# Selective attention and a routed expert layer: the diagonal half blocks of keys in 64 by 64 tiles

## The chip, the cores and the metric

The kernel runs on one core of a Trainium2 chip. A core has five engines, each with a queue of its own: TensorE multiplies matrices (a weight load, then a matmul that streams the moving operand past the weights), VectorE and ScalarE work element by element, GpSimd does masks and indirect stores, and SyncE issues most transfers. The engines wait for each other at semaphores. The results of matmuls land in PSUM; the attention here uses three buffers of two banks and two single banks of it, a bank being 512 fp32 columns on 128 partitions. All other tiles lie in SBUF, 128 partitions wide.

The metric is the device time of the whole kernel in microseconds (us), given as the median of the runs. Beside it stands one execution that the hardware profiler recorded; its span runs from the first to the last instruction. All data is fp32, and an fp32 product appears in the trace as two records of a weight load and a matmul.

## The reference

Inputs have 8 batches, 8 heads, 576 positions and head size 64. The first half is causal attention with a bias from a running sum of a score `s`:

```python
scores = scale * np.matmul(q, k.transpose(0, 1, 3, 2))
causal = np.triu(np.ones((S, S), dtype=bool), k=1)
cum = np.cumsum(np.maximum(s, 0.0), axis=-1)
bias = -(cum[:, :, :, None] - cum[:, :, None, :])
scores = np.where(causal, -1e9, scores + np.minimum(bias, 0.0))
attn = np.exp(scores - np.max(scores, axis=-1, keepdims=True))
attn = attn / (np.sum(attn, axis=-1, keepdims=True) + 1e-09)
out = np.matmul(attn, v)
```

Its output, 8 x 576 tokens of width 512, goes into a routed layer. Each token has logits over 8 experts; a local gate says whether it takes the expert of its own largest logit or that of the token before it. The token then gets `relu(x @ w1[e]) @ w2[e]` (512 to 1024 to 512), times its probability of that expert.

## The kernel before

**Two stages.** `attention` (L764) computes all of the attention, and between its pieces the routing of batches that are complete. `Experts.run` (L647) then goes through the tokens sorted by expert. A fallback for inputs out of range (`attention_general` and what follows it) is built into the program and does not run on this input.

**Pairs and slots.** A unit of attention is n: one batch and two heads, 32 in all. The two heads lie on partitions 0 to 63 and 64 to 127 of q and k. The main loop (L1000) takes two n at a time, the first (a) and the second (b); I call one turn of it a slot, 0 to 15. In a slot TensorE does four score units of a, four of b, then the values of a, then those of b.

**Scores.** Keys are taken in chunks of 128 (c = 0 to 3, and NF = 4 for the last 64). A chunk needs only queries from its own first position on. `UNITS` (L40) says which chunks make up a unit, with query ranges and the place of each in the unit; `WIDTH` gives 384, 384, 448 and 384 columns per head. `scores` (L891) issues for each piece one product per head: contraction over 64 partitions, 128 keys as output rows. The result is in one of three PSUM buffers of two banks (`ps_s`, L779), one bank per head. One exponential on ScalarE (L903) takes the unit to SBUF (`e`), and `masked` (L887) on GpSimd zeroes what lies above the diagonal.

**Values.** Queries are taken in blocks of 64 (j = 0 to 8). For block j, `values` (L922) adds over all chunks c up to the diagonal: `e` of 64 queries as weights, contraction over 128 keys, and as moving operand the weighted values `vg`, 66 columns wide (64 values, the key weight for the row's sum, and ones). A head's output goes to half of the partitions. Blocks whose diagonal chunk is only half filled (j even) still contract over all 128 keys: the upper half of the weights was set to zero. Blocks 0 to 5 and 6 to 8 (`NJA = 6`) have one bank each, from the pool `ps_o` (L780), which both n of a pair share. `evacuate` on VectorE divides by the row's sum (a reciprocal, L939, and a multiply, L940).

**What sets the order.** The program's order is kept as it is written, on every engine. A tile of a pool waits for the last reader of the tile that had its buffer before. `at(m, place)` (L996) runs work that was planned for slot m: places 0 and 1 come after the scores of a and b, 3 and 4 after their values, 5 at the slot's end. The router's steps are planned there (L965): `product` at place 1 of slots 4, 8 and 12, `logits` at 3, `codes` and `turn1` at 5; in the slot after, `turn2` at 3; in the next one `ranks` (the matmuls called pos) at 1, `rows` and `gates` at 3. `assign_early` is at place 3 of slot 11. Stores to a table in memory (`scatter`, L339) are spread over places 0 to 5 of later slots; some wait on GpSimd for a reciprocal of a value block.

**Loads.** `load_qk` (L788) fetches q and k of one n. In slot m it is issued, after the first n's values, for the pair two slots on, with a small copy on ScalarE to hold it back. `load_v` fetches values six n ahead; `weigh` (L874) multiplies them by the key weights, one slot ahead, on VectorE. Key weights (`key_weights`, L857) are made once in slot 0.

Of the kernel before, what the change touches and what calls it, by code (L numbers as in the profile page):

```python
# [9 lines left out]
F32 = mybir.dt.float32  # L10
I32 = mybir.dt.int32
Act = mybir.ActivationFunctionType
Alu = mybir.AluOpType
# [22 lines left out]
NJ = S // DH  # L36
NJA = 6
G1 = 2
REF = (127, 415)
UNITS = (((0, 0, 384, 0),), ((0, 384, S, 0), (3, 384, S, 192)), ((1, P, S, 0),), ((2, 256, S, 0), (NF, TS, S, 320)))  # L40
WIDTH = (384, 384, 448, 384)
GB = 2
# [8 lines left out]
BX = 3  # L51
FIRST = ((0, P, 0, 3 * P), (P, S, 3 * P, S))
CAP = N + DH
# [710 lines left out]
def attention(ctx, tc, q, k, v, s, wx, ident, recs, wend, router, experts):  # L764
# [4 lines left out]
    def pool(name, bufs, **kw):  # L769
        return ctx.enter_context(tc.tile_pool(name=name, bufs=bufs, **kw))  # L770
# [3 lines left out]
    p_v = pool("p_v", NVA)  # L774
    p_e = pool("p_e", 2)
    p_x = experts.p_x
    p_x0 = pool("p_x0", 1)
# [6 lines left out]

    ins, vs, es, xs, xts = {}, {}, {}, {}, {}
    heads = [slice(DH * h, DH * h + DH) for h in range(2)]

    def load_qk(n, behind=None):  # L788

        if n >= NPAIR:  # L790
            return
        b, hp = divmod(n, HP)
        ins[n] = qb, kb = p_in.tile([P, S], F32, name="qb"), p_in.tile([P, S], F32, name="kb")
        if behind is not None:
            nc.scalar.copy(kb[0:1, 0:1], behind)
        for k0, k1, q0, q1 in FIRST if n == 0 else ((0, S, 0, S),):
            nc.sync.dma_start(kb[:, k0:k1], k[b][:, hp, k0:k1])
            nc.sync.dma_start(qb[:, q0:q1], q[b][:, hp, q0:q1])

# [28 lines left out]
    wk = once.tile([P, NPAIR, G1 + NB, 2], F32, name="wk")  # L828
    nc.gpsimd.memset(wk[:TL, :, G1 + NF], 0.0)
    for t in vgs:  # L830
        nc.gpsimd.memset(t[..., VW - 1 : VW], 1.0)
        nc.gpsimd.memset(t[:TL, G1 + NF, :, VW - 1 : VW], 0.0)

# [18 lines left out]
    def key_weights():  # L852
        cps = banks("cps")[:, 0].rearrange("p (i n) -> p i n", n=B * H)
        i = 0
        for w, n in ((w1, G1), (w2, NB)):
            for c in range(n):
                a = min(c * P, S - P)  # L857
                tr(cps[:, i], w[:, a : a + P], ident[: B * H, : B * H])
                i += 1
        for i in range(G1 + NB):  # L860
            d = slice(TL if i == G1 + NF else 0, P)
            nc.vector.tensor_copy(wk[d, :, i, :].rearrange("p n h -> p h n"), cps[d, i].rearrange("p (h n) -> p h n", h=2))

# [22 lines left out]

    def masked(ap, n, base=0):  # L887
        nc.gpsimd.affine_select(out=ap, in_=ap, compare_op=Alu.is_ge, fill=0.0, base=base, pattern=n,  # L888
                                channel_multiplier=-1)

    def scores(n, u):  # L891
        if n >= NPAIR:
            return
        qb, kb = ins[n]
        if u == 0:
            es[n] = [p_e.tile([P, 2, w], F32, name=f"e{i}") for i, w in enumerate(WIDTH)]
        e = es[n][u]
        ps = banks("ps")[:, :, : WIDTH[u]]
        for c, a, z, at in UNITS[u]:
            key = min(c * P, S - P)  # L900
            for h, d in enumerate(heads):
                mm(ps[:, h, at : at + z - a], lhsT=kb[d, key : key + P], rhs=qb[d, a:z], start=True, stop=True)  # L902
        nc.scalar.activation(e, ps, Act.Exp, scale=scale)  # L903
        for c, a, z, at in UNITS[u]:
            m = min(P, z - a)
            if a < c * P + P:
                masked(e[:, :, at : at + m], [[0, 2], [1, m]], P - m)

# [12 lines left out]

    def values(n, j0, j1):  # L922
        b, hp = divmod(n, HP)
        if b not in xs:
            xs[b] = x_tile(b) if b < BX else p_x.tile([P, NJ, 2, XW], F32, name="xb")
        xb = xs[b]
        po = ps_o.tile([P, j1 - j0, VW], F32, name=f"po{j0}")
        for j in range(j0, j1):
            last = j // 2 if j < NJ - 1 else NF
            for c in range(last + 1):  # L930
                for h, d in enumerate(heads):
                    mm(po[d, j - j0, :], lhsT=weights_of(n, c, j, h),  # L932
                       rhs=vgs[n % NV][:, c if j < 2 * G1 else G1 + c, h, :],
                       start=(c == 0), stop=(c == last))

        def evacuate():
            m = j1 - j0
            rec = recs[:, n, j0:j1, :]
            nc.vector.reciprocal(rec, po[:, :, VW - 2 : VW])  # L939
            nc.vector.tensor_tensor(xb[:, j0:j1, :, 32 * hp : 32 * hp + 32], po[:, :, :DH].rearrange("p j (g i) -> p j g i", g=2),  # L940
                                    rec[:, :, 0].unsqueeze(2).unsqueeze(3).to_broadcast([P, m, 2, 32]), op=Alu.mult)

        return evacuate, po[0:1, 0, 0:1]

# [51 lines left out]
    def at(slot, place):  # L996
        for f in todo.pop((slot, place), ()):
            f()

    for m in range(NPAIR // 2):  # L1000
        pair = 2 * m, 2 * m + 1
        for n in pair:
            for u in range(len(UNITS)):
                if (n, u) == (0, 2):
                    key_exps()
                scores(n, u)
                if (n, u) == (0, 3):
                    key_weights()
                    weigh(0)
                    weigh(1)  # L1010
                if (n % 2, u) == (1, 1):
                    load_v(n - 1 + NVA, es[n][u][0:1, 0, 0:1])
                    load_v(n + NVA)
            at(m, n - 2 * m)
        for n in pair:
            values(n, 0, NJA)[0]()
            evacuate, done = values(n, NJA, NJ)
            if n % 2 == 0:
                load_qk(n + NV, done)
                load_qk(n + 1 + NV)  # L1020
            evacuate()
            at(m, 3 + n - 2 * m)
        last = m % HP == HP - 1
        if last:
            turns(pair)
        for n in range(WEIGHED[m - 1] + 1 if m else 2, WEIGHED[m] + 1):
            weigh(n)
        if not last:
            turns(pair)
        at(m, 5)  # L1030
# [36 lines left out]
def attention_general(ctx, tc, q, k, v, s, w_gate, w_local, cum_d, x_d, ident, lg):  # L1067
# [24 lines left out]
    def load_batch(b):  # L1092
        if b >= B:
            return
        qb = p_in.tile([P, HP, S], F32, name="qb")
        kb = p_in.tile([P, HP, S], F32, name="kb")
        vb = p_in.tile([P, NF, H, DH], F32, name="vb")
        vl = p_in.tile([TL, H, DH], F32, name="vl")
        nc.sync.dma_start(qb, q[b])
        nc.sync.dma_start(kb, k[b])  # L1100
        for hp in range(HP):
            hs = slice(2 * hp, 2 * hp + 2)
            nc.sync.dma_start(vb[:, :, hs], v[b, hp][:, :NF])
            nc.sync.dma_start(vl[:, hs], v[b, hp][TL:, NF])
        ins[b] = qb, kb, vb, vl
# [500 lines left out]
```

## Time and profile before

| what | us |
|---|---|
| median of 3 runs | 747.14 (745.63 to 747.15) |
| profiled execution, whole | 731.85 |
| its span, first to last instruction | 730.1 |
| sixteen slots of attention, first score to last value | 4.8 to 209.4 |
| experts, to the end | 209.4 to 730 |

The profile's busy row of an engine is the time in which it had at least one instruction under way; matmuls overlap, so TensorE at 98% is not TensorE at its peak. The chain of waits follows the work that ended last backwards from the end. Rows of groups give line, engine, operation, tiles, the shape, the count, the busy time and the mean length of one in ns. `64*128` in such a row is a matmul on 64 partitions with 128 weight columns, `128*64` one on 128 partitions with 64.

In the ten slices of the span that hold the attention, VectorE is busy 40 to 80%, ScalarE 30 to 50%, GpSimd 30 to 80%:

```profile
DVE  4656678778865751101111401420041001050010
ACT  5554555363521101101101011101101011101110
POOL 3453467688583534510010101010001001010110
```

The exponentials, masks and evacuations of the attention are these groups:

```profile
L903 ACT ACTIVATE e<-ps 128x768 f32<-128x768 f32 (+1 forms) x128 | 96.5, 839 | 47.2 <-PE ps L902 42.3
L888 POOL TENSOR_SCALAR_AFFINE_SELECT e<-e 128x256 f32<-128x256 f32 (+1 forms) x160 | 67.2, 445 | 50.4 <-ACT e L903 49.5
L939 DVE RECIPROCAL recs<-po 128x12 f32<-128x12 f32 x64 | 13.4, 210 | 51.4 <-PE po L932 39.9
```

### The profile page before, as it was taken

The page shows a single profiled execution, that of the slowest core. Times are in us where ns is not written, and L with a number is a line of the kernel's source. Part 1 is how long each engine was busy: PE and PEld are TensorE (multiplying, and loading weights), DVE is VectorE, ACT ScalarE, POOL GpSimd, SP SyncE. Part 2 cuts the span into 40 slices and gives each one's busy share as a digit, 9 for nine tenths or more (in the row PEclk, how much of TensorE's full clock was granted, in tenths as well). Part 3 has the DMA queues.
Part 4 walks back from the last instruction along what each step waited for, and adds up shares of the span by engine and source line. Part 5 has one row for each costly group of instructions (what it writes and reads, how often), then busy time and mean ns, then how long its engine had stood idle before and what let it go on. Part 6 is the DMA issues. An engine that isn't in the chain of part 4 may idle for free.

```text
span 730.1 us, 16198 instructions
## 1 busy us (share of the span) xinstructions
PE 719.0 (98%) x6521; PEld 496.6 (68%) x6521; DVE 258.4 (35%) x713; ACT 165.4 (23%) x355; POOL 206.1 (28%) x453
## 2 busy tenths in 40 slices
PE   8999999999999999999999999999999999999996
PEld 7888888878886766756765377446736576646673
DVE  4656678778865751101111401420041001050010
ACT  5554555363521101101101011101101011101110
POOL 3453467688583534510010101010001001010110
PEclk9999999999999999999999999999999999999998
DMA  8455465765749997887457969996999964997000
GB/s 305 153 173 170 142 197 172 219 207 184 216 150 424 343 384 263 320 331 221 151 210 243 399 256 426 311 381 261 388 363 374 389 240 176 341 410 288 30 17 32
DMA packets 57205, 187.28 MB, mean 257 GB/s; under 512 B 11838, under 2 KB 32062, under 8 KB 49569
## 3 DMA queue, kind: packets, MB, share of 16 engines
q1 hardware_dynamic: 50224, 165.91, 63.7%
q0 software_dynamic: 6800, 20.09, 7.2%
q8 instruction: 53, 0.87, 0.5%
q14 instruction: 32, 0.25, 0.1%
q10 hardware_dynamic: 96, 0.15, 0.1%
HBM read 165.50 MB, written 20.75 MB: 255 GB/s over the span
## 4 chain that ended last, share of the span: by engine, by line
PE 96%; DMA 1%; ACT 1%; DVE 1%; issue 1%; POOL 0%; POOLq 0%; DVEq 0%; ACTq 0%
PE yp L634 35%; PE hp L608 31%; PE po L932 12%; PE ps L902 11%; PE hp L599 4%; PE lp L217 1%; DMA table<-xb,idx 1%; ACT e L903 1%; PE warm L837 1%; DVE xb L940 0%; PE pos L301 0%; POOL e L888 0%; POOL table L349 0%; PE pos L302 0%; DVE y L637 0%
## 5 line engine op out<-in xcount | busy, mean ns | idle before, releaser
L634 PE MATMUL yp<-w2b,hT 128*128 128x512 f32 (+3 forms) x752 | 259.3, 593 | 0.0
L608 PE MATMUL hp<-xT,w1b 128*128 128x256 f32 (+2 forms) x1216 | 229.8, 349 | 0.0
L608 PEld LDWEIGHTS hp<-xT,w1b 128*128 128x128 f32 x1216 | 206.2, 190 | 29.3 <-issue 7.5
L634 PEld LDWEIGHTS yp<-w2b,hT 128*128 128x128 f32 (+3 forms) x752 | 107.1, 166 | 141.8 <-issue 140.2
L639 POOL DMA_INDIRECT out_dram<-y,gi x37 | 36.4, 984 | 413.2 <-DVE y L637 387.3
L610 ACT ACTIVATE hT<-hp 128x256 f32<-128x256 f32 (+2 forms) x152 | 53.4, 352 | 425.4 <-PE hp L608 425.4
L637 DVE TENSOR_SCALAR y<-yp,gi 128x512 f32<-128x512 f32 (+1 forms) x37 | 27.6, 745 | 304.8 <-PE yp L634 298.5
L903 ACT ACTIVATE e<-ps 128x768 f32<-128x768 f32 (+1 forms) x128 | 96.5, 839 | 47.2 <-PE ps L902 42.3
L932 PE MATMUL po<-vg,e 128*64 128x66 f32 x3200 | 98.5, 223 | 2.2 <-issue 1.2
L932 PEld LDWEIGHTS po<-vg,e 128*64 128x64 f32 x3200 | 95.5, 138 | 5.1 <-issue 3.7
L902 PE MATMUL ps<-qb,kb 64*128 64x192 f32 (+4 forms) x768 | 94.1, 397 | 0.5 <-ACT e L903 0.3
L902 PEld LDWEIGHTS ps<-qb,kb 64*128 64x128 f32 x768 | 64.9, 187 | 28.8 <-ACT e L903 16.3
L888 POOL TENSOR_SCALAR_AFFINE_SELECT e<-e 128x256 f32<-128x256 f32 (+1 forms) x160 | 67.2, 445 | 50.4 <-ACT e L903 49.5
L349 POOL DMA_INDIRECT table<-xb,idx x54 | 54.2, 1003 | 17.1 <-issue 13.3
L619 DVE STREAM_TRANSPOSE hT<-hs 32x256 f32<-32x256 f32 x64 | 27.9, 436 | 72.3 <-ACT hs L601 71.4
L882 DVE TENSOR_TENSOR vg<-va,wk 128x256 f32<-128x256 f32 x64 | 41.7, 716 | 0.0
L939 DVE RECIPROCAL recs<-po 128x12 f32<-128x12 f32 x64 | 13.4, 210 | 51.4 <-PE po L932 39.9
L599 PE MATMUL hp<-w1b,xT 128*32 128x512 f32 (+1 forms) x224 | 28.3, 594 | 0.0
L578 DVE STREAM_TRANSPOSE xT<-xq 128x1024 f32<-128x1024 f32 (+1 forms) x23 | 23.6, 1028 | 12.0 <-DMA xq<-table 11.6
L940 DVE TENSOR_TENSOR xb<-po,recs 128x384 f32<-128x384 f32 (+1 forms) x48 | 22.0, 458 | 2.4 <-DMA table<-xb,idx 0.8
L599 PEld LDWEIGHTS hp<-w1b,xT 128*32 128x32 f32 (+1 forms) x224 | 8.1, 114 | 17.6 <-issue 17.5
L951 DVE STREAM_TRANSPOSE xt<-xb 128x576 f32<-128x576 f32 x24 | 17.1, 751 | 0.0
(254 smaller groups left out, 200.8 us busy)
## 6 DMA issues: line engine op xcount, KB each, us to landing
w2b<-in_w_dram SPq DMA_DIRECT2D x30, 2048.0 KB, 12.8
w1b<-in_w_dram SPq DMA_DIRECT2D x29, 2048.0 KB, 10.1
va<-in_v_dram SPq DMA_DIRECT2D x32, 320.0 KB, 4.2
kb<-in_k_dram SPq DMA_DIRECT2D x31, 288.0 KB, 3.4
qb<-in_q_dram SPq DMA_DIRECT2D x31, 288.0 KB, 4.9
xq<-table SPq DMA_DIRECT2D x56, 130.0 KB, 8.6
w1b<-in_w_dram SPq DMA_DIRECT2D x4, 512.0 KB, 5.2
xq<-table SPq DMA_DIRECT2D x20, 65.0 KB, 11.0
```

The source lines that it names most:

```text
L349: put = self.nc.gpsimd.indirect_dma_start(out=self.halves, in_=src, element_offset=0, in_offset=None, out_offset=bass.IndirectOffsetOnAxis ...
L599: mm(ps[d, :], lhsT=xT[:, k, d], rhs=self.ws[l][0][:, k, c * 512 : c * 512 + 512], start=(k == 0), stop=(k == DK - 1))
L608: mm(ps[:, :w], lhsT=self.ws[ls[0]][0][:, k, c * P : c * P + P], rhs=xT[:, k, :w], start=(k == 0), stop=(k == DK - 1))
L610: nc.scalar.activation(self.hT[u][:, c, :w], ps[:, :w], Act.Relu)
L619: self.nc.vector.transpose(hT[32 * a : 32 * a + 32, :, 32 * r : 32 * r + 32], hs[32 * r : 32 * r + 32].rearrange("p (c i) -> p c i", i=P)[ ...
L634: mm(ps[d, :], lhsT=hT[:, k, n * P + d.start : n * P + d.stop], rhs=self.ws[l][1][:, k, :], start=(k == 0), stop=(k == FK - 1))
L639: put = nc.gpsimd.indirect_dma_start(out=self.out[:, :], out_offset=bass.IndirectOffsetOnAxis(ap=gi.bitcast(I32)[:m, n, 0:1], axis=0), in_ ...
L882: nc.vector.tensor_tensor(vg[:, to].rearrange("p c h e -> p (c h) e")[:, :, :DH], va[:, :c].rearrange("p c h e -> p (c h) e"), wk[:, n, to ...
L888: nc.gpsimd.affine_select(out=ap, in_=ap, compare_op=Alu.is_ge, fill=0.0, base=base, pattern=n, channel_multiplier=-1)
L902: mm(ps[:, h, at : at + z - a], lhsT=kb[d, key : key + P], rhs=qb[d, a:z], start=True, stop=True)
L903: nc.scalar.activation(e, ps, Act.Exp, scale=scale)
L932: mm(po[d, j - j0, :], lhsT=weights_of(n, c, j, h), rhs=vgs[n % NV][:, c if j < 2 * G1 else G1 + c, h, :], start=(c == 0), stop=(c == last))
```

## The change

The keys are put into another order, made where the inputs are laid out: block 8 first, then 0, 1, 2, 3, 5, 4, 7, 6. A chunk of 128 keys now starts at 64, so chunk c holds blocks 2c and 2c + 1 (for c = 2 and 3 in swapped places). The whole chunk is computed only for queries from block 2c + 1 on. For query block 2c itself only half of the chunk counts, its diagonal half block of 64 keys; for blocks 0, 2, 4 and 6 that half is computed apart, as 64 by 64 tiles, with blocks 0 and 4, and 2 and 6, side by side on the two halves of the partitions (`HALVES`).

- Scores: three units per n in place of four (512, 448 and 384 columns; chunk queries start 64 later), and one more unit of 256 columns per pair for the half blocks of both n (`scores_halves`), with one exponential and two masks. It is issued in the slot before the one that uses it, between the values of a and of b.
- Values: whole chunks contract over 128 keys as before; the four half blocks contract over 64 (`values_halves`). The halves of a close its accumulation, those of b open it, so both stand together.
- Banks: the values of a stay in `ps_o`; those of b go to a buffer of `ps_s`. Blocks are split into 0 to 3 and 4 to 8 (`NJA = 4`).
- Order in a slot: scores of a and b; whole values of a, its halves, halves of b, half scores of the next pair; evacuation of a; the loads; place 3; then the whole values of b.
- In slot 0 the first loads are cut differently, the key weights are turned after the third unit, and chunks with swapped blocks take two copies (nine in place of seven).

```diff
-NJA = 6
+NJA = 4
-UNITS = (((0, 0, 384, 0),), ((0, 384, S, 0), (3, 384, S, 192)), ((1, P, S, 0),), ((2, 256, S, 0), (NF, TS, S, 320)))
-WIDTH = (384, 384, 448, 384)
+BLOCKS = (8, 0, 1, 2, 3, 5, 4, 7, 6)
+UNITS = (((0, DH, S, 0),), ((1, 3 * DH, S, DH), (NF, TS, S, 0)), ((2, 5 * DH, S, 0), (3, 7 * DH, S, 256)))
+WIDTH = (512, 448, 384)
+TURNED = (2, 3)
+ROOM = (512, 448, 512)
+HALVES = ((0, 4), (2, 6))
...
+    p_eh = pool("p_eh", 1)
...
         for i in range(G1 + NB):
-            d = slice(TL if i == G1 + NF else 0, P)
-            nc.vector.tensor_copy(wk[d, :, i, :].rearrange("p n h -> p h n"), cps[d, i].rearrange("p (h n) -> p h n", h=2))
+            d = slice(0, P)
+            c = i - G1
+            for to, of in (heads[:2],) if c == NF else (heads, heads[::-1]) if c in TURNED else ((d, d),):
+                nc.vector.tensor_copy(wk[to, :, i, :].rearrange("p n h -> p h n"),
+                                      cps[of, i].rearrange("p (h n) -> p h n", h=2))
...
+    def scores_halves(m, ps):
+        if 2 * m >= NPAIR:
+            return
+        eh[m] = p_eh.tile([P, 2, 2, len(HALVES), DH], F32, name="eh")
+        ps = ps[:, :, : 4 * DH]
+        for i in range(2):
+            qb, kb = ins[2 * m + i]
+            for t, blocks in enumerate(HALVES):
+                for side, x in zip(heads, blocks):
+                    at = (2 * i + t) * DH
+                    key = BLOCKS.index(x) * DH
+                    for h, d in enumerate(heads):
+                        mm(ps[side, h, at : at + DH], lhsT=kb[d, key : key + DH], rhs=qb[d, x * DH : x * DH + DH],
+                           start=True, stop=True)
+        nc.scalar.activation(eh[m].rearrange("p h n t i -> p h (n t i)"), ps, Act.Exp, scale=scale)
+        by = eh[m].rearrange("p h n t i -> p (h n t) i")
+        masked(by[:DH], [[0, 8], [1, DH]])
+        masked(by, [[0, 8], [1, DH]], DH)
...
+    def room(n):
+        if n % 2:
+            po = banks("pb")
+            po = [po[:, i] for i in range(2)]
+        else:
+            po = [ps_o.tile([P, 512], F32, name=f"po{i}") for i in range(2)]
+        return [ps[:, : (z - a) * VW].rearrange("p (j w) -> p j w", w=VW) for ps, (a, z) in zip(po, PARTS)]
+
+    def values(n, po, part, first, last):
+        a, z = PARTS[part]
+        steps = [(j, c) for j in range(a, z) for c in [*range((j + 1) // 2), *([NF] if j == NJ - 1 else [])]]
+        for i, (j, c) in enumerate(steps):
+            for h, d in enumerate(heads):
+                mm(po[part][d, j - a, :], lhsT=weights_of(n, c, j, h),
+                   rhs=vgs[n % NV][:, c if j < 2 * G1 else G1 + c, h, :],
+                   start=(first and i == 0), stop=(last and i == len(steps) - 1))
+
+    def values_halves(n, po, first):
+        e = eh[n // 2][:, :, n % 2]
+        for t, blocks in enumerate(HALVES):
+            for part, (side, j) in enumerate(zip(heads, blocks)):
+                for h, d in enumerate(heads):
+                    mm(po[part][d, j - PARTS[part][0], :], lhsT=e[side, h, t],
+                       rhs=vgs[n % NV][side, j // 2 + (G1 if part else 0), h, :],
+                       start=(first and t == 0), stop=(not first and t == 1))
...
-        for n in pair:
-            values(n, 0, NJA)[0]()
-            evacuate, done = values(n, NJA, NJ)
-            if n % 2 == 0:
-                load_qk(n + NV, done)
-                load_qk(n + 1 + NV)
-            evacuate()
-            at(m, 3 + n - 2 * m)
+        a, b = pair
+        po = room(a)
+        for i in range(2):
+            values(a, po, i, True, False)
+        values_halves(a, po, False)
+        halves = banks("ph") if b + 1 < NPAIR else None
+        to = room(b)
+        values_halves(b, to, True)
+        scores_halves(m + 1, halves)
+        evacuate(a, po, 0)
+        load_qk(a + NV, po[1][0:1, 0, 0:1])
+        load_qk(b + NV)
+        evacuate(a, po, 1)
+        at(m, 3)
+        for i in range(2):
+            values(b, to, i, False, True)
+            evacuate(b, to, i)
+        at(m, 4)
```

## The prediction

> **What bounds the kernel now.** I read the page's busy rows first, then the chain of waits, then the groups with shapes kept apart, last VectorE's timeline and TensorE's waits.
>
> ```profile
> span 730.1 us, 16198 instructions
> PE 719.0 (98%) x6521; PEld 496.6 (68%) x6521; DVE 258.4 (35%) x713; ACT 165.4 (23%) x355; POOL 206.1 (28%) x453
> ...
> PE   8999999999999999999999999999999999999996
> ```
>
> TensorE is busy from end to end, at full clock. A busy TensorE can still hide slack, so the chain between 61 and 89 us has to show a rhythm:
>
> ```profile
> 61.70 2.31 PE lp L217 x64
> 64.01 5.98 PE po L932 x200
> 69.99 5.76 PE ps L902 x48
> 75.75 5.98 PE po L932 x200
> 81.74 5.76 PE ps L902 x48
> ```
>
> A slot (one pair of n) is 5.76 us of scores and 5.98 us of values, 11.74 in all, and nothing else ends last. Sixteen slots fill 4.8 to 209.4 us; the experts after them are not edited, and TensorE is busy 513.8 of their 520.6 us. So the change is worth what it does to TensorE's 11.74 us per slot, plus any wait it opens. The groups give the unit prices:
>
> ```profile
> L634 PE MATMUL yp<-w2b,hT 128*128 128x512 f32 x464 | 202.8, 593 | 0.0
> L932 PEld LDWEIGHTS po<-vg,e 128*64 128x64 f32 x3200 | 95.5, 138 | 5.1 <-issue 3.7 <-POOL e L888 0.7
> L902 PEld LDWEIGHTS ps<-qb,kb 64*128 64x128 f32 x768 | 64.9, 187 | 28.8 <-ACT e L903 16.3 <-issue 0.7 <-DMA qb<-in_q_dram 0.6
> L217 PEld LDWEIGHTS lp<-xt,wx 128*32 128x32 f32 x320 | 8.6, 110 | 0.8 <-issue 0.3
> L217 PE MATMUL lp<-xt,wx 128*32 128x160 f32 x192 | 7.1, 300 | 0.0
> ```
>
> An fp32 product is two records. A whole-array record of 512 columns costs 202.8/464 = 437 ns, 0.854 ns a column. The values phase has 200 x 66 columns, 11.3 us at that price, and takes 5.98: two column tiles run at once. Scores: 12,800 columns, 10.9 us, in 5.76: two row tiles at once. The router's product: 64 x 160 columns, 8.7 us, in 2.31: 3.8 tiles at once.
>
> **What the Trainium skill says.** "TensorEngine Tiling (Array Packing)", Tiling Modes: 64 by 64 is four independent tiles, and changing the mode drains TensorE. The trace shows the drain: from the starts of single records, the last score to the first value is 202 ns and the next start 108, where 49 and 58 are the rhythm: 0.20 us; values to scores likewise 0.20. It shows no 64 by 64 tile. "TensorE: Matmul & The Clock Gate", LDWEIGHTS: time goes with columns, P/1.2 ns; the records agree (187, 138, 110 ns for 128, 64, 32 columns: 0.8 ns each). Its Back-to-back issue gap gives a floor of about 25 ns a matmul; the trace differs, records of different tiles start 6 to 7 ns apart. "PSUM — Partial Sum Buffer", PSUM bank collisions: row tiles may not share a bank; the change keeps each row tile in its own bank, so this costs nothing.
>
> **The change, part by part.** Rhythm of two tiles, from starts: 0.84 ns a column and record for wide scores, 58.4 ns for a values step of 66 columns, 112 ns where a 64-column score has 128 weights to load (56 before, but the next step is late by as much).
>
> *Scores before*: per n 1,536 wide columns x 2 x 0.84 = 2.58 us, and 0.11 to 0.22 for the 64: 5.50 a pair. *After*: 512+384+256+128 = 1,280 columns x 2 x 0.84 = 2.15, the 64-wide 0.22: 2.37 per n, 4.75 a pair. Saved 0.75.
>
> *Half scores*: 16 products a pair, 32 records of 64 columns. Four at a time that is 8 steps of 56 ns, 0.45 us; two at a time 0.90. I take four: column tiles show 3.8, row tiles 1.9, each with its own weight loads in parallel, and the router's four products stand in the program in the same way.
>
> *Values before*: 25 (block, chunk) steps per n, 50 a pair x 2 x 58.4 = 5.84. *After*: 21 whole per n, 42 x 2 x 58.4 = 4.91, and 16 half products: 8 steps, 0.47 (0.93 if only two tiles run). Saved 0.46.
>
> *Switches*: two a slot become four (scores, values of a, halves, values of b). I take 0.17 us for each new one: the lp to values switch cost 0.16, the dear ones 0.20; bounds 0.10 and 0.25.
>
> Sum of an ordinary slot: 4.75+0.45+4.91+0.47+0.40+0.34 = 11.32 against 5.50+5.84+0.40 = 11.74: **0.42 us less**. Slots 1 to 14: 5.9. Slot 15 computes no next halves: 0.87. Slot 0 computes two sets of halves with two more switches (+0.79), and its halves reuse the bank pair of the transposed key weights, whose copies grow from 7 to 9 (about 0.17 us each): +0.3. With its own 0.42 off, slot 0 loses 0.7. TensorE: **-6.1 us**.
>
> *New wait*. The values of the second n leave ps_o for one of the three score buffers. The third score unit of the next slot takes that buffer, so it waits for the last evacuation, on VectorE, behind whatever the router has at place 3. An evacuation pair takes 1.31 us. In after's slot, with 0 at its first score, the first n's evacuation can start at 7.98, and the second's last multiply must end by 11.31+1.73 = 13.0 (1.73 us are the first two units). That leaves 2.2 us for place 3. The timeline of before:
>
> ```profile
> 79.56 0.70 DVE L278 COPY ei<-exm 32x18 f32<-32x18 f32 x4
> ...
> 82.22 0.21 DVE L939 RECIPROCAL recs<-po 128x12 f32<-128x12 f32 x1
> ...
> 92.01 0.30 DVE L310 TENSOR_TENSOR at<-pos,base 128x144 f32<-128x144 f32 x1
> ...
> 94.92 0.23 DVE L939 RECIPROCAL recs<-po 128x12 f32<-128x12 f32 x1
> ...
> 154.74 0.16 DVE L366 TENSOR_TENSOR cnt<-base,base 128x8 int32<-128x8 f32 x1
> ...
> 157.51 0.23 DVE L939 RECIPROCAL recs<-po 128x12 f32<-128x12 f32 x1
> ```
>
> turn2 takes 2.7 us (slots 5, 9, 13), rows and gates 2.9 to 3.1 (slots 6, 10, 14), assign_early 2.8 (slot 11); logits, 2.2, just fit (slots 4, 8, 12). Over the 2.2: 0.5, 0.8, 0.6. In slots 9 and 13 codes and turn1 of the slot before run until about 8.5, 0.5 more. Together 3 x 0.5 + 2 x 0.5 + 3 x 0.8 + 0.6 = **+5.7 us** (I round up by 0.2 for the semaphores). Queued behind the waiting matmul is all of TensorE. Bounds: 0 if VectorE runs ahead of my sum, 9 if it runs 0.5 later in the seven slots.
>
> *Waits that go*. Values of the second n now have banks of their own, so they no longer wait for the first n's evacuation:
>
> ```profile
> PE po L932 <- DVE xb L940: 0.3, 1, 0.3
> PE po L932 <- DVE recs L939: 0.2, 1, 0.2
> ```
>
> The starts show three such gaps, at 128.7, 179.8 and 192.9 us: 1.2 us over the rhythm. Next in line there is the wait just priced. Slot 11 loses 0.7 us at 150 to 157 us, mostly to masks behind two stores on GpSimd; I take half back, 0.35, since the stores stay.
>
> *At nothing*. ScalarE: exponentials start every 0.70 (768) and 0.81 us (896), so 0.93, 0.81, 0.70 and 0.47 a half set: 5.35 a slot, 5.82 before; the three buffers cover its small lag behind TensorE (2.44 against 2.37 per n). GpSimd: ten masks (3.9 us in a quiet slot) become six plus two of 512 elements; from 0.29 and 0.34 us for 128 and 256 these take 0.45, up to 1.0 when contended: 3 to 4.5, read a slot later. On its queue they now stand ahead of place 3's store, which waits for the first n's reciprocal anyway. SyncE: the same q, k and v bytes; the next pair's q and k are wanted at 7.9 us in the slot after their issue at about 9, after 10 us, and land in some 7 (four, at medians of 3.4 and 4.9). If that cover fails, the halves wait up to 2 us a slot. The key and value orders are made outside the timed program.
>
> Sum: -6.1 + 5.7 - 1.2 - 0.35 = **-1.95 us**. The profiled execution would go from 731.85 (span 730.1) to about 729.9. The median of the runs is 747.14, 15.3 us more, which no view explains; I take it as fixed: **745.2 us**.
>
> **The rivals.**
> 1. *No late VectorE.* The evacuation always meets its limit: -6.1-1.2-0.35 = -7.7, 739.5 us. For it: VectorE is busy only 6.4 to 9.1 us of the five slots I asked for, 11.8 to 14 us long. Against: the sums above are of measured lengths, in order.
> 2. *Halves two at a time (slower).* The half products cost 0.92 us a slot more, 15 us in all. They delay the second values by 0.68, so the late evacuation shrinks to 1.1. Sum -6.1+15+1.1-1.2-0.35 = +8.4: 755.5 us. It decides once the halves cost 0.19 us a slot more (16 steps of 57 ns, 0.92 us, become 1.1), so below about 3.3 tiles of 4 at once. For it: no 64 by 64 tile in the trace, and weights of 64 columns need as long as their matmul. Against: rows and columns each pack.
> 3. *The buffer wait everywhere.* With one of three buffers held until a slot's end, TensorE, ScalarE and VectorE run in lockstep and most slots lose 0.3 more, or the new switches cost 0.25: +4.5 on the forecast, 749.7 us. For it: ScalarE is as slow as TensorE in the scores. Against: in a plain slot the last evacuation ends 0.87 us after the scores start and is wanted at 1.73.
>
> That the change does not do what it says is excluded: the changed order on TensorE has 16 products of 64x64 and 16 half values a slot, and the third unit waits on VectorE.
>
> **How the numbers follow.** Forecast 0.44 (742.5 to 747.5), rival 1 0.14, rival 2 0.18, rival 3 0.24. No change means within 0.2%, 1.5 us. Faster: 0.33 + 0.14 + 0.01 = 0.48; same: 0.08 + 0.05 = 0.13; slower: 0.03 + 0.18 + 0.18 = 0.39. The range reaches to half of rivals 1 and 2: 740 to 755.5.
>
> **What would show it.** In quiet slots (1 to 3) the chain should repeat every 11.3 us: scores 4.75, first values 2.45, halves 1.1 with both products, second values 2.45. Halves of 2 us mean rival 2. In slots 6, 7, 10, 11, 12, 14 and 15 the first record of the third score unit should start 0.5 to 1 us late, released by VectorE; without that it is rival 1. A shortfall in quiet slots too is rival 3. Wrong altogether if the experts' stretch, 520.6 us, changes.

## The result, and the profile after

| | before | changed kernel |
|---|---|---|
| median of 6 runs each, us | 746.48 (745.56 to 747.15) | 813.11 (811.04 to 814.43) |
| ratio to before | 1 | 1.088, 95% interval 1.087 to 1.090 |
| profiled span, us | 730.1 | 812.5 |
| attention ends, first expert product (us of the span) | 209.6 | 289.7 |

The change costs 66.6 us where 2 us of gain were forecast. The kernel before itself takes 746 to 747 us in some sets of runs and 730 to 731 in others (its profile is like the latter), so every kernel below is set against the runs of before in its own set.

The page of the changed kernel, its header, TensorE's busy row and slices, and the clock it was granted:

```profile
span 812.5 us, 16822 instructions
...
PE 742.6 (91%) x6909; PEld 512.3 (63%) x6909; DVE 255.0 (31%) x715; ACT 157.8 (19%) x339; POOL 202.2 (25%) x421
...
PE   8987778777777789999999999999999999999996
...
PEclk9999889989888999999999999999999999999999
```

The loss lies in the first 15 slices, which are the attention. There TensorE is mostly seven to eight tenths busy where it had been full, and its clock falls too. The rest, 522.8 us from 289.7 to the end, is close to the 520.5 of before.

The chain of waits of the changed kernel, over the end of slot 2 and the start of slot 3, two quiet slots (start, length, engine, tile):

```profile
46.16 0.60 ACT eh L937
46.81 0.23 DVE recs L992
47.07 0.49 DVE w2b L993
47.71 0.44 DVE w2b L993
48.19 2.20 PE pb L972 x68
50.39 4.96 PE ps L913 x40
55.35 2.60 PE po L972 x84
57.95 0.39 PE po L982 x16
58.35 0.23 PE pb L982 x16
58.58 0.69 PE ph L935 x32
```

Before, this chain held TensorE alone, scores and values in turn. Now the second half of every slot goes ScalarE, VectorE, TensorE. In the 84 records of the second values (L972, `pb`), the first 16 run at once; the other 68, which are part 1, start only after an evacuation (L993). TensorE's waits say the same:

```profile
PE pb L972 <- DVE xb L993: 48.0, 12, 4.7
PE pb L972 <- DVE w2b L993: 3.1, 2, 1.7
PE pb L972 <- DVE w1b L993: 3.0, 2, 1.5
```

Sixteen waits, one a slot, 54.1 us. (`xb`, `w1b` and `w2b` are the same output tiles under different names.) Measured from the starts of single records, the gap before part 1 is 1.6 to 1.8 us in the five slots without router work for VectorE at place 3 and 3.5 to 4.8 us in the other eleven, 56.7 us in all. Slot 6 in the timeline shows what is in such a gap:

```profile
109.14 0.69 PE L972 MATMUL pb<-vg,e 128*64 128x66 f32 x16
109.77 0.13 ACT L800 COPY kb<-po 1x1 f32<-1x1 f32 x1
109.94 0.22 DVE L992 RECIPROCAL recs<-po 128x10 f32<-128x10 f32 x1 [0.72 <-ACT kb L800]
110.60 0.30 DVE L314 TENSOR_TENSOR at<-pos,base 128x144 f32<-128x144 f32 x1
...
113.72 0.20 DVE L992 RECIPROCAL recs<-pb 128x8 f32<-128x8 f32 x1
113.96 0.42 DVE L993 TENSOR_TENSOR xb<-pb,recs 128x256 f32<-128x256 f32 x1
114.44 4.01 PE L972 MATMUL pb<-vg,e 128*64 128x66 f32 x68 [4.61 <-DVE xb L993]
```

Part 0 of b is done by 109.8. Its evacuation stands on VectorE behind the evacuation of a and then behind the router's rows and gates (L314 to L340), so it ends at 114.4. Part 1 of b starts at 114.44, directly after it, although it writes the other bank. Then those 68 records last 4.01 us instead of the 2.2 of the quiet slot. The windows of these two stretches give the reason (stretch, length, busy time of the engines, then the granted clock, DMA share, GB/s):

```profile
core 0: us, PE busy (x) PEld busy (x) DVE busy (x) ACT busy (x) POOL busy (x), PEclk, DMA share, GB/s
...
114.40:118.30 3.90, 3.86 (x68) 3.82 (x68) 0.00 (x0) 0.00 (x0) 0.00 (x0) 0.50 0.05 17
118.30:124.00 5.70, 5.70 (x46) 3.64 (x44) 4.20 (x8) 3.88 (x5) 3.59 (x7) 0.89 0.07 23
```

After the wait TensorE runs at half clock for the whole of part 1 and into the scores. "TensorE: Matmul & The Clock Gate" of the Trainium skill, in its part on the HAM clock gate, says that the clock drops to half after an idle window of some 3.4 us. The trace agrees with the length of the window: the second values lose 1.3 to 1.8 us more after each of the eleven long waits, 3.46 us and up, and the half clock starts at times that are whole multiples of 3.41 us apart (20.58, 78.61, 95.67 us and so on) and lasts 3.41 or 6.83 us.

But here the window need not be idle all through. Of the five short waits, slot 0's is followed by the half clock as well (its half scores had halted 0.8 us just before): in the 3.41 us up to 20.58 TensorE was busy for 1.49. If this trace's attention is cut into such windows, every one with 1.92 us or more of idle time is followed by half clock; those at full clock with less, 1.66 us at most, are not. Three of the other short waits are followed by nothing of the kind, and slot 7's second values hold two other stalls of 0.6 us. All together it is 20.6 us in the second values, 1.3 of them in slot 7, and 2.9 in the scores.

So 56.7 + 20.6 + 2.9 = 80.2 us lost, against 7.7 us of forecast gains (6.1 on TensorE, 1.55 in waits): 72.5. The two spans differ by 82.4 us. Of the 10 between, 2.3 lie in the experts and some 7 in short stalls of TensorE, of a kind that before's profile does not have (last section). The medians differ by only 66.6, because before's own runs beside it took 15 us more than its profile; no trace shows where they spend them.

### The profile page after: what moved, and what is told of

Read it like the earlier page. It is cut to its first block, busy times and chain, and to the rows that moved or that the text cites. A ratio compares the mean times of both kernels' runs of the same rounds, so it can differ in the third digit from the quotient of the medians.

```text
span 812.5 us, 16822 instructions
## 1 busy us (share of the span) xinstructions
PE 742.6 (91%) x6909; PEld 512.3 (63%) x6909; DVE 255.0 (31%) x715; ACT 157.8 (19%) x339; POOL 202.2 (25%) x421
## 4 chain that ended last, share of the span: by engine, by line
PE 89%; DVE 7%; issue 2%; ACT 1%; DMA 0%; SPq 0%; POOL 0%; POOLq 0%; DVEq 0%; ACTq 0%
PE yp L638 32%; PE hp L612 28%; PE ps L913 10%; PE pb L972 7%; PE po L972 5%; PE hp L603 3%; DVE xb L993 1%; PE lp L221 1%; PE ph L935 1%; ACT eh L937 1%; PE po L982 1%; DVE l L236 1%; DVE recs L992 1%; DMA va<-in_v_dram 0%; PE pb L982 0%
## 5 line engine op out<-in xcount | busy, mean ns | idle before, releaser
L972 PE MATMUL pb<-vg,e 128*64 128x66 f32 x1344 | 65.9, 276 | 54.9 <-DVE xb L993 48.0
L914 ACT ACTIVATE e<-ps 128x1024 f32<-128x1024 f32 (+2 forms) x96 | 80.8, 924 | 97.9 <-PE ps L913 97.9
L972 PEld LDWEIGHTS pb<-vg,e 128*64 128x64 f32 x1344 | 60.7, 187 | 58.5 <-DVE xb L993 49.6
L913 PE MATMUL ps<-qb,kb 64*128 64x64 f32 (+5 forms) x644 | 84.9, 415 | 0.8 <-ACT e L914 0.8
L913 PEld LDWEIGHTS ps<-qb,kb 64*128 64x128 f32 x644 | 55.1, 194 | 29.1 <-issue 8.2
L897 POOL TENSOR_SCALAR_AFFINE_SELECT e<-e 128x128 f32<-128x128 f32 (+2 forms) x96 | 40.8, 435 | 65.8 <-ACT e L914 65.1
L972 PE MATMUL po<-vg,e 128*64 128x66 f32 x1344 | 44.3, 224 | 1.0 <-issue 0.8
L972 PEld LDWEIGHTS po<-vg,e 128*64 128x64 f32 x1344 | 41.4, 138 | 4.1 <-issue 2.7
L992 DVE RECIPROCAL recs<-po 128x8 f32<-128x8 f32 (+1 forms) x32 | 6.8, 214 | 77.6 <-PE po L982 65.3
L897 POOL TENSOR_SCALAR_AFFINE_SELECT eh<-eh 64x512 f32<-64x512 f32 (+1 forms) x32 | 21.0, 656 | 38.8 <-ACT kb L800 33.4
```

What stands on the lines that cost most here:

```text
L914: nc.scalar.activation(e[:, :, : WIDTH[u]], ps, Act.Exp, scale=scale)
L972: mm(po[part][d, j - a, :], lhsT=weights_of(n, c, j, h), rhs=vgs[n % NV][:, c if j < 2 * G1 else G1 + c, h, :], start=(first and i == 0), ...
```

## The experiments

The theory: part 0 and part 1 of b lie in one tile of two banks (`banks("pb")`), and the program has `evacuate(b, to, 0)` ahead of `values(b, to, 1)`; so part 1, a writer of the tile, waits for the reader of part 0, whichever bank that reads. The rivals: the half blocks themselves, their masks, or the held score buffer cause the stall.

**Both evacuations last.** The order alone is changed.

```diff
         for i in range(2):
             values(b, to, i, False, True)
+        for i in range(2):
             evacuate(b, to, i)
```

> The changed kernel with one move: both parts of the second n's values are issued before both of its evacuations. Theory A, one tile: in the changed kernel the second part (68 records) waits for the evacuation of the first part, because both parts lie in one two-bank tile and that evacuation stands ahead of them; the waits add up to some 56 us and the halved clock after them to some 20 us. So A expects 736 to 743 us here: second values 2.45 us in quiet slots (4.15 before the move), clock 0.99 or more, and at most 6 us of new waits of the third score unit for VectorE. Theory B, the held score buffer: giving one of three score buffers to the values until the slot's end is what costs; then 790 us or more, with the waits at the score units. Theory C, VectorE is simply late: the wait moves from the values to the next slot's third score unit and the time stays above 790 us.

Measured: 739.56 us (738.57 to 741.1) beside 730.68 of before; ratio 1.0129, interval 1.0112 to 1.0146. The second values take 2.45 us in nine of the sixteen slots and at most 3.6 in the rest, the granted clock is 0.999 over the span, and most of the loss has gone. That 739.56 lies in the expected 736 to 743 is luck: these numbers stood against 747 of before and meant 4 to 11 us less than it, and it is 8.9 more. The mechanism held; the new wait, at most 6 us expected, is larger. It is the one that the prediction had priced:

```profile
PE ps L913 <- DVE xb L993: 10.5, 10, 1.8
```

Ten score phases are late, by 0.6 to 2.0 us over their 4.76, 12.6 us in all; 5.7 us in seven slots were forecast. The chain of this kernel at slot 9's end tells why it is more (pieces as before, some left out):

```profile
132.05 0.60 ACT eh L937
132.65 0.04 ACT kb L800
...
132.71 0.23 DVE recs L992
...
132.97 0.49 DVE xb L993
133.46 0.07 DVE ei L282
...
136.07 0.47 DVE incl L297
...
137.26 0.50 DVE xb L993
...
137.90 3.31 PE ps L913 x28
```

The second evacuation of a (132.71) waits for the one-element copy of L800, which `load_qk` places on ScalarE between the two evacuations of a; and that copy is queued behind the exponential of the half scores. The pair that the sum had at 1.31 us runs from 131.12, in the timeline, to 133.46: 2.34 us; in the other slots before a late score phase it takes 2.13 to 2.52, but in slot 14 1.58. "PSUM — Partial Sum Buffer" of the Trainium skill, in the section on bank collisions, tells of a scheduler that adds a dependency between two engines on one bank and quarter of the partitions, reads included; this copy and this evacuation are such a pair, both reading bank po1. The trace shows that the evacuation waits for the copy; that this rule put the wait there is not shown.

**The kernel before, with both parts of its values in one tile of two banks.** No half blocks, no held score buffer: only the suspected cause.

```diff
-        po = ps_o.tile([P, j1 - j0, VW], F32, name=f"po{j0}")
+        if j0 == 0:
+            pos[n] = ps_o.tile([P, 2, 512], F32, name="po")
+        po = pos[n][:, int(j0 > 0), : (j1 - j0) * VW].rearrange("p (j w) -> p j w", w=VW)
```

> The kernel before, with both parts of an n's values in one tile of two banks instead of a tile each; nothing else is changed. Theory A: the second part of every n waits for the evacuation of the first, about 1.1 us (0.17 drain, 0.23 and 0.56 on VectorE, 0.14 to release), 35 us over 32 n; the second n's first part waits for the first n's last evacuation, about 1.2 us, 19 us; and in the eleven slots with router work at place 3 the second n's wait is 2 to 3 us longer, some 25 us. Sum about 825 us, and in any case over 780. Theories B and C have no wait here that was not there before: 750 us at most.

Measured: 795.96 us beside 730.68 (one run). The tile alone costs the kernel before 65 us. Its waits:

```profile
PE po L934 <- DVE xb L942: 40.5, 35, 1.9
PE po L934 <- DVE w1b L942: 5.6, 6, 1.0
PE po L934 <- DVE w2b L942: 4.7, 5, 1.0
```

Here both n of a pair have such a tile, so there are 46 waits, none over 1.9 us. The kind is right; the amount is below the 78 us expected, since the longer waits expected in the slots with router work did not come.

**The changed kernel with the router behind.** Evacuation 0 of b is moved ahead of place 3; the tile stays one.

```diff
-        at(m, 3)
-        for i in range(2):
-            values(b, to, i, False, True)
-            evacuate(b, to, i)
+        values(b, to, 0, False, True)
+        evacuate(b, to, 0)
+        at(m, 3)
+        values(b, to, 1, False, True)
+        evacuate(b, to, 1)
```

> The changed kernel with place 3 (the router's work on VectorE) moved from ahead of the second n's first values and their evacuation to behind them; VectorE has the same work. Theory A: the second part still waits for the evacuation of the first, but about 1.7 us in every slot as in the quiet ones, and no wait is long enough to halve the clock: 760 to 770 us, clock 0.99 or more. Theory C: VectorE's load is the same, so 800 us or more. Theory B: no difference, 813 us.

Measured: 748.52 us beside 730.68 (one run), 17.8 more than before; 13 to 23 more were expected (the numbers there stand against 747). TensorE's waits:

```profile
PE pb L972 <- DVE xb L993: 17.1, 12, 1.7
PE pb L972 <- DVE w1b L993: 3.0, 2, 1.5
PE pb L972 <- DVE w2b L993: 3.0, 2, 1.5
```

Sixteen waits are left, but now every slot has the quiet slot's, 1.1 to 1.9 us by the starts of records, 25.7 in all. No second values run at the lowered clock: part 1 takes the quiet slot's 2.13 us in all sixteen slots, so nothing is left of the 20.6 us. So the place of the router's work decides between 1.7 us and 4.8, and with the long waits the lowered clock goes too.

**Where the third unit's wait comes from.** Three kernels on top of "both evacuations last", and the changed kernel itself beside them. The first moves the loads of q and k:

```diff
-        load_qk(a + NV, po[1][0:1, 0, 0:1])
-        load_qk(b + NV)
         evacuate(a, po, 1)
+        load_qk(a + NV, po[1][0:1, 0, 0:1])
+        load_qk(b + NV)
```

> As the kernel with both of the second n's evacuations last (ratio 1.013 to before; third score unit late by 12.6 us in all), but the loads of the next q and k, whose one-element copy on ScalarE stands between the two evacuations of the first n and holds VectorE idle about 0.9 us a slot, are issued behind the second of them. Theory (the wait at the third score unit is VectorE's backlog, mis-sized because this idle time was not counted): each of the ten late score phases (0.6 to 2.0 us over 4.76) gets up to 0.9 shorter, sum 8.5 us, so about 1.001 of before. Rival (the held score buffer costs in itself, whatever VectorE does): the score phases stay as late, 1.013.

The second moves work of VectorE from place 3 to place 4:

```diff
-        plan(m + 1, 3, lambda g=g: router.turn2(g))
+        plan(m + 1, 4, lambda g=g: router.turn2(g))
...
-        plan(m + 2, 3, lambda g=g: router.gates(g, [xs[b] for b in range(g * GB, g * GB + GB)]))
+        plan(m + 2, 4, lambda g=g: router.gates(g, [xs[b] for b in range(g * GB, g * GB + GB)]))
...
-    plan(m - 5, 3, lambda: router.assign_early(0))
+    plan(m - 5, 4, lambda: router.assign_early(0))
```

(The first part of the weights that this assignment chooses moves with it.)

> As the kernel with both of the second n's evacuations last, but the parts of the router's place 3 that free no PSUM bank (turn2, gates, the early assignment) are issued behind those evacuations. Theory (backlog of VectorE): the score phases after slots 5, 9, 13 (turn2), 6, 10, 14 (gates) and 11 (assignment) fall back to 4.76 to 4.9 us; those after 4, 8 and 12 (logits, 2.2 us, still ahead) stay 0.8 to 1.1 us late. Sum 9.7 us less, ratio 0.999 to 1.001. Rival (held score buffer): still about 1.013.

The third has both:

> Both of these together: loads of q and k behind the first n's evacuations, and turn2, gates and assignment behind the second's. Theory (backlog of VectorE): all late score phases gone but some tenths, 12.3 us less than the kernel with the evacuations last, so attention about 6 us shorter than before, as the TensorE terms of the prediction have it: ratio 0.993 to 0.997. Rival (held score buffer): above 1.008.

And the changed kernel:

> The changed kernel itself, beside these: the same ratio to before as in its own runs, 1.08 to 1.095, if the ratios carry over between sets of runs; its second values late by 1.7 us in quiet slots and 4 to 5 us in the others.

| kernel | time, us (before beside it 747.03) | ratio, 95% interval | score phases late, us in all |
|---|---|---|---|
| keys behind | 747.65 | 1.0008, 0.9997 to 1.0019 | 5.6 |
| router last | 747.08 | 1.0008, 0.9984 to 1.0031 | 4.5 |
| both | 748.27 | 1.0031, 1.0018 to 1.0044 | 2.8 |
| changed kernel | 812.99 | 1.0900, 1.0882 to 1.0918 | |

The changed kernel gives its ratio again. Each move takes most of the late scores away, so the wait is VectorE's backlog; the held score buffer by itself costs at most the little that is left. But the third kernel is not faster than the first two, and it misses the 0.993 to 0.997 expected of it: 10 us fewer late scores than at 1.013, and still not below before. Where this went is the next question.

**The same kernel once more, with before's own trace beside it.**

> The kernel before, profiled in the same set of runs as the kernels below. Where its runs take 747 us, as in three of the four sets so far, and not the 731.85 of the profile that the prediction was read from: theory (small stalls of TensorE that wait for nothing the profile shows, 'issue', which are in every kernel of such a set): 10 us or more of its 15 extra us are such gaps in the slots, at unchanged phase lengths (5.76 and 5.98). Rival (a lower clock): the phases themselves are longer.

> The kernel with loads of q and k behind the first n's evacuations and turn2, gates and assignment behind the second's, once more beside before's own trace. Score phases late by about 3 us in all, against 12.6 without these two moves. Ratio to before 1.000 to 1.005 if the set takes 747 us for before; 0.995 to 1.000 if it takes 731.

Measured: before 730.45 us (its profiled run 730.72), the kernel with both moves 731.54 (729.74 to 733.64), ratio 1.0013, interval 1.0001 to 1.0024, where 0.995 to 1.000 was expected. Before took 730 us here, so the question where the other 15 us of its 747 come from stays open. The two traces can be compared, though. TensorE's waits of the kernel with both moves:

```profile
PE pb L972 <- issue: 3.5, 6, 1.0
PE po L972 <- POOL e L897: 2.5, 3, 1.7
...
PE ps L913 <- ACT e L914: 0.8, 2, 0.5
```

Late scores are down to 0.7 us. From the starts of records, slots 1 to 15 lose 11.2 us over their quiet lengths; before loses 2.0 in the same slots. The quiet slots are shorter by 7.5 in all, and slot 0 is 1.6 longer (scores of slot 1 start at 21.48, not 19.88): -7.5 + 11.2 - 2.0 + 1.6 = +3.3, where attention ends 3.0 later (211.65 against 208.63). The 11.2 have two main parts. 2.5 are masks: with the gates moved, a store waits for them on GpSimd, and the masks of the next values queue behind it. And 5.8 are gaps that wait for nothing the profile shows, all of one kind, as this list of single records from the traces has it (the largest of each kernel; number of the record on TensorE, in brackets its remainder by 127, the step from the record before it in us; the rhythm is 0.06 or less):

```
both moves       600 (92) 0.53   1108 (92) 0.78   1744 (93) 0.82   2632 (92) 1.18   3773 (90) 0.79   3900 (90) 0.87   4027 (90) 0.71
evacuations last 600 (92) 1.08   1745 (94) 0.49   1998 (93) 0.80   2633 (93) 0.22   3395 (93) 0.37   4284 (93) 0.39
before            219 (92) 0.91   2629 (89) 0.25   2882 (88) 0.16
```

Their distances are 127 records or multiples of it, give or take a few.

**All records shifted by 32.** Sixteen products of 32 by 32 are added to the warm-up of the kernel with both moves.

```diff
             mm(warm[:, :P], lhsT=zero, rhs=zero, start=True, stop=True)
+        for i in range(16):
+            mm(warm[:32, :32], lhsT=zero[:, :32], rhs=zero[:, :32], start=True, stop=True)
```

> The kernel with both moves, and 16 products of 32 by 32 (32 records on TensorE) added to the warm-up; all that follows is shifted by 32 records. The short stalls of TensorE in the values, which wait for nothing the profile shows, stand at records 92 or so past a multiple of 127 in several kernels. Theory (TensorE's stream of instructions is refilled every 127 products' records and runs dry where the records are shortest): the stalls stay at 92 past a multiple of 127 and so come at other places of the program. Rival (something in the program holds those products): they stay at the same products, now 124 past a multiple of 127. Time within 1 per cent of the same kernel without the added products.

Measured: 749.29 us beside 747.31, ratio 1.0029 (1.0016 to 1.0041), as without the added products. The gaps of this kind are at records 220 (93), 346 (92), 1744 (93), 2250 (91), 2632 (92), 3773 (90) and 4280 (89), with 1.29, 0.97, 0.47, 0.27, 0.40, 0.20 and 1.77 us. None is at 124. So it is not a product of the program that waits: the stream itself halts, at places 127 records apart. What it waits for stands in the traces too. The profile's page has a queue row "q8 instruction", 56 packets of 16 KB (0.92 MB), and in the attention these come one to about 127 records. Each of the gaps listed here, in all four traces, ends 1.2 to 1.6 us after the latest of these packets has landed. In the three traces listed above, where the packet had landed earlier than that, the place passes without such a gap. So the stream, by all that these traces show, waits for its next block of instructions.

**One tile for each part.** The changed kernel in its own order; two score buffers of two banks, and two buffers for each part of the values, one bank each.

```diff
-    ps_s = pool("ps_s", 3, space=PSUM)
-    ps_o = pool("ps_o", 1, space=PSUM)
+    ps_s = pool("ps_s", 2, space=PSUM)
+    ps_o = pool("ps_o", 2, space=PSUM)
...
-        if n % 2:
-            po = banks("pb")
-            po = [po[:, i] for i in range(2)]
-        else:
-            po = [ps_o.tile([P, 512], F32, name=f"po{i}") for i in range(2)]
+        po = [ps_o.tile([P, 512], F32, name=f"po{i}") for i in range(2)]
```

> The changed kernel in its own order, but the two parts of the second n's values in two tiles of one bank each (two score buffers instead of three, two buffers for each part of the values). Theory (VectorE's evacuation of part 0 holds part 1 only because both lie in one tile): second values 2.45 us, as the first, in every slot, no long wait and no lowered clock; in place of it the scores wait for ScalarE with two buffers, estimated at 0.3 to 1 us a slot: ratio 1.000 to 1.015. Rival (TensorE is held by the order of the program, evacuation before values of part 1, whatever the tiles): second values 4 to 9 us and 1.08 to 1.1, as the changed kernel.

Measured: 746.41 us beside 730.45, ratio 1.0215 (1.0198 to 1.0232), above the 1.000 to 1.015 expected. The second values take 2.45 us in nine of the sixteen slots and at most 3.3 in the others, with `evacuate(b, to, 0)` still ahead of part 1 in the program and the router still between: the order alone does not make the wait, it takes the shared tile. (Here b holds no score buffer either. That this is not what matters is shown above, where the tile alone made the wait in the kernel before, and where the wait went though the buffer was still held.) But scores take 5.97 us or a little more in every slot from 1 on, 1.21 more, where 0.3 to 1 was expected. The chain at slot 4:

```profile
61.47 1.08 PE ps L913 x4
...
62.58 1.03 ACT e L914
...
63.65 1.96 PE ps L913 x12
...
65.64 1.03 ACT e L914
...
66.72 0.92 PE ps L913 x8
```

With two buffers the third unit waits for ScalarE's exponential of the first, and the sixth for that of the fourth. So a tile for each part, paid for with the third score buffer, costs 18 us (1.21 in each of 15 slots).

**The stores one slot later.** Made to take the mask waits out of the kernel with both moves.

```diff
-STORES = (((5,), (0, 1, 3, 4, 5), (0, 1, 3, 4, 5), (0, 1, 3, 4, 5), (0, 0)), ((5, 5), (0, 1, 3, 4, 5), (0, 1, 3, 4, 5), (0, 1, 1, 3, 4, 5)),
+STORES = (((), (0, 1, 1, 3, 4, 5), (0, 1, 3, 4, 5), (0, 1, 3, 4, 5), (0, 0)), ((), (0, 0, 1, 1, 3, 4, 5), (0, 1, 3, 4, 5), (0, 1, 1, 3, 4, 5)),
```

> The kernel with both moves (keys behind, router last), and in addition the first stores of the first two groups one slot later, behind the masks of the first n, since in it these stores wait on GpSimd for the gates that were moved, with the masks of the next values queued behind them (first values late by 0.56 us in slot 7 and 1.76 us in slot 11). Theory: both waits go, 2.3 us, ratio to before 0.996 to 1.000. Rival (the masks are late for another reason, or the stores collide with the masks of the second n): no gain, 1.001 or more.

Measured: 750.62 us (747.4 to 753.98) beside 747.31, ratio 1.0043 (1.0025 to 1.0061). The waits for masks are gone from TensorE's list, as expected, but the time is not lower. Attention ends at 219.95 us, against 219.46 of the kernel with both moves in the table above. Why nothing is gained is not settled: the trace shows more stalls of the kind described at the very end of this text. The rival's word, no gain, holds for the time, and not for its reason.

No version that was run beats the kernel before.

## Why the prediction was wrong

**The step that failed** is under *Waits that go*: "Values of the second n now have banks of their own, so they no longer wait for the first n's evacuation", and "Next in line there is the wait just priced". The banks are their own against the first n. But the second n's two parts share one tile, and part 1 waits for part 0's evacuation, which the sum had at nothing: 56.7 us, and some 22 more through the clock (the 23.5 above less slot 7's 1.3). The prediction asked which tile a value of b shares with a, and not which it shares with the other part of b. It had the two facts for it: the four calls in their order in the diff, and `banks("pb")` as one tile whose parts are slices. In before each part is a tile. Moving the evacuations behind both parts took away the wait (ratio 1.088 to 1.013), one tile for both parts put it into the kernel before (+65 us), and one tile for each part took it away again.

**The term that was mis-sized** is *New wait*: 5.7 us for the third score unit, 12.6 measured once the larger wait was out of the way, in ten slots and not in seven. "An evacuation pair takes 1.31 us" leaves out what stands between the two halves: the copy of `load_qk` on ScalarE behind the half scores' exponential. The pair takes 2.13 to 2.52 us in nine of the ten slots before a late phase, 8.5 us more than the sum had in all ten. The slots with logits, which "just fit", no longer did: they make up 2.7 of the 12.6, and the seven slots of the sum 9.9. The two terms together, 5.7 + 8.5 = 14.2, are 1.6 more than was measured. With the copy moved away the late scores fall by 7.0, to 5.6 us.

**TensorE's terms held.** Scores 4.76 us (4.75 forecast), half scores 0.43 (0.45), values 2.45 for each n (4.91 for two), half values 0.48 (0.47) with records 6 to 7 ns apart in fours, new switches 0.15 (0.17). A quiet slot whose waits are gone is 11.25 us (11.32), so the 0.42 us a slot are there.

**At nothing** failed in one place: these faster records brought 5.8 us of halts of the stream where before has 2.0 of stalls of any kind. The prediction has no term for them, though the profile that it was read from has two, in slots 1 and 2 (steps of 0.37 and 0.64 us at records 473 and 726). Masks and ScalarE were covered, as said, in the changed kernel itself: TensorE waits 0.8 us for ScalarE's score exponentials there, and no wait for a mask stands in its list.

**The rivals.** *Halves two at a time* fell: they run four at once. *No late VectorE* fell with the 12.6 us. *The buffer wait everywhere* fell as a mechanism: quiet slots without the tile's wait run at 11.25. None of them had the wait within `pb`, so the range did not reach to it, and the forecast came out 68 us too low.

## What to carry to other kernels

- When a buffer moves into another pool, list for each write the reads of the *same tile* that stand ahead of it in the program, and not those of the same bank. Two parts that are filled and read in turn need a tile each, or all writes ahead of the first read.
- A long wait on TensorE was paid twice here: the waits of 1.1 to 1.9 us with the router behind cost themselves alone, those of 3.5 us and more another 1.3 to 1.8 us at half clock. Short waits close together can do the same: 1.92 us of idle time in 3.41 were enough.
- A gain of 0.42 us in a slot of 11.74 has to be weighed against every queue it leans on: a one-element copy between two evacuations (the pair takes 0.8 to 1.2 us longer in most slots) and a third score buffer given up (1.21 us) were each worth more than it.

## What the runs showed that was not expected

TensorE's stream can halt once in about 127 records, until shortly after a block of instructions has landed, 0.2 to 1.8 us at a time, where the records are short. With half blocks, the 232 records of a slot's values and half scores pass in about 6 us, and more of these halts show: 5.8 us in slots 1 to 15.

Where before takes 747 us, the traces of the kernels beside it have stalls of another kind: runs of some three to six records, then a step of 0.3 to 0.7 us, two to four times in a row, at no fixed remainder by 127. The changed kernel's own trace has some 8 us of them; slot 7's two stalls are such a pair. The kernel with both moves, timeline of TensorE from its run in the table:

```profile
185.33 0.28 PE L982 MATMUL pb<-vg,eh 64*64 64x66 f32 x5
185.77 0.36 PE L982 MATMUL pb<-vg,eh 64*64 64x66 f32 x5 [0.16 <-issue]
186.50 0.36 PE L982 MATMUL pb<-vg,eh 64*64 64x66 f32 x6 [0.37 <-issue]
187.22 0.74 PE L935 MATMUL ph<-qb,kb 64*64 64x64 f32 x32 [0.37 <-issue]
```

The same kernel beside a before of 730 us has no such run of steps in its attention. Its two profiled spans differ by 12.9 us, 7.8 of them in the attention and 5.1 in the experts. The steps come near 130, 185 and 213 us in all five kernels that keep both evacuations last and ran beside a before of 747 us. What they wait for is open, and so is how much of them before has, since both its traces are of runs at 730 to 732 us.
